# Upper weights of two matrix products placed 64 and 32 bytes beyond the common rest by 2048

## The chip, the cores and the metric

The kernel runs on one core of a Trainium2 chip. The metric is device time in microseconds, the median of several runs. A core has a matrix engine (TensorE, PE in the profile; its loads of the stationary operand are listed as PEld), a vector engine (VectorE, DVE), a scalar engine (ScalarE, ACT), a general engine (GpSimd, POOL) and a queue engine that starts DMAs (SyncE, SP). All read operands from the on-chip memory SBUF, which has 128 partitions; an address below is the byte within a partition, the same for all partitions.

## The reference

Attention in a sliding window of 64 positions, then a feed-forward layer with a normalized SoLU. Batch 8, 8 heads, 576 positions, head size 64; 4608 tokens, model width 512, hidden width 1024.

```python
def _attn_ref(q, k, v):
    scores = scale * np.matmul(q, k.transpose(0, 1, 3, 2))
    mask = (rel >= 0) & (rel < 64)
    scores = np.where(mask, scores, -1000000000.0)
    attn = softmax(scores)          # exp, sum, divide
    return np.matmul(attn, v)

def _moe_ref(x, w_in, w_out, g_ln):
    h = x @ w_in                    # 4608 x 512 @ 512 x 1024, the first product
    solu = h * softmax(h)
    ln = (solu - mean) / np.sqrt(var + 1e-06) * g_ln
    return ln @ w_out               # 4608 x 1024 @ 1024 x 512, the second product
```

## The kernel before

The tokens are cut into 36 tiles of 128. For each tile the kernel computes the scores (line 460), the softmax, the transposed probabilities, the attention's values (line 559), the first product (`moe_in`), the normalization (`moe_norm`), a transpose, and the second product (`moe_out`). All operations of all tiles go into a planner (`Plan`), which orders them by costs and due times that are written into the source; each engine's instructions are then emitted in that order. The planner knows no addresses.

The products run in three passes at a reduced 32-bit float form (`F32R`): an operand is split into an upper part, rounded to that form, and a lower part, the rest. The three passes are upper x upper, upper x lower and lower x upper. The first three tiles of the first product and the first two of the second run in plain fp32 instead (lines 590 and 724), while the split weights are still being made.

- Upper weights: `w_inH` ([128, 4, 1024], first product) and `w_outH` ([128, 8, 512], second product), 16384 bytes in each partition, both in the pool `const`. ACT writes them once (lines 392 and 397).
- Lower weights: `WL(i)`, eight of the sixteen uses of the ring `w` (nine tiles of 4096 bytes each); its other eight uses hold the weights in plain fp32.
- Activations: `xH`, `xL` (2048 bytes a tile), `yH`, `yL` (4096 bytes a tile), upper and lower, in rings of two.

In a matmul the activations are the stationary operand: 128 columns, 512 bytes in each partition, loaded by an instruction of their own (PEld). The weights are the moving operand: 512 columns, 2048 bytes, streamed past. For each pair of output halves (first product) or input chunks (second product) the order of passes is a group of six:

```python
        passes = [(c, d, *kinds[k]) for c in range(NC) for d, k in ((0, 0), (0, 1), (1, 0), (1, 1), (0, 2), (1, 2))]
```

so the streamed weights go upper, lower, upper, lower, upper, upper. In the first product `xH[:, c]` is the stationary operand of the first four and `xL[:, c]` of the last two. There are four groups per tile, 24 matmuls, in each product. Line 603 issues those of the first product, line 737 those of the second; 33 tiles go through line 603 and 34 through line 737.

Tiles lie in SBUF in the order in which they are first asked for: first the pool `const`, then the rings of the pool `sb` (`qk`, `raw`, `v`, `sS`, `w`, `PT`, `xH`, `e`, `sq`, `yH`, `xL`, `ot`, `yL`, `y`), then small columns. Two tiles of `const` are never used, `shift` and `gap`; they only take room:

```python
    const.tile([P, 272], F32, name="shift")
    w_inH = const.tile([P, NC, DFF], F32R, name="w_inH")
    w_outH = const.tile([P, NF, DM], F32R, name="w_outH")
    g_sb = const.tile([P, NF], F32, name="g_sb")
    const.tile([P, 240], F32, name="gap")
    neghalf = const.tile([P, 1], F32, name="neghalf")
```

`g_sb` holds the layer's scale, read when the second product's weights are split; `neghalf` is a constant of 4 bytes.

Of the kernel before, what the change touches and what calls it, by code (L numbers as in the profile page):

```python
# [9 lines left out]
F32 = mybir.dt.float32  # L10
# [9 lines left out]
P = 128  # L20
# [206 lines left out]
def tile_window_attention_solu_moe(  # L227
# [31 lines left out]
    const = ctx.enter_context(tc.tile_pool(name="const", bufs=1))  # L259
# [24 lines left out]
        if first is not None:  # L284
            nc.gpsimd.memset(t[first * WIN:(first + 1) * WIN, :WIN], NEG)

    const.tile([P, 272], F32, name="shift")
    w_inH = const.tile([P, NC, DFF], F32R, name="w_inH")
    w_outH = const.tile([P, NF, DM], F32R, name="w_outH")
    g_sb = const.tile([P, NF], F32, name="g_sb")  # L290
    const.tile([P, 240], F32, name="gap")
    neghalf = const.tile([P, 1], F32, name="neghalf")
    nc.gpsimd.memset(neghalf, -0.5)

# [605 lines left out]
```

## Time and profile before

| | |
|---|---|
| Median of three runs | 512.38 us (511.92 to 512.64) |
| Profiled execution, its own time | 513.01 us |
| Its span, first to last instruction | 510.9 us |
| PE busy | 492.1 us (96%), 4064 matmuls |
| PEld busy | 392.4 us (77%) |
| DVE busy | 409.8 us (80%) |
| ACT busy | 355.6 us (70%) |
| POOL busy | 314.5 us (62%) |
| DMA | 94.09 MB, 184 GB/s on average |
| Granted PE clock | 1.00 |

Busy times of different engines overlap, so they do not add up to the span. Matmuls overlap one another as well: the time that a matmul adds is the distance from its start to the next one's start (its pitch), not its listed duration. A group in the profile is named by source line, engine, operation, and output<-inputs.

### The profile page before, as it was taken

How to read it: one execution, taken by the hardware profiler on the slowest of the kernel's cores; microseconds unless marked ns; L12 is line 12 of the kernel's file. 1: busy time of each engine (PE TensorE's matmuls, PEld its weight loads, DVE VectorE, ACT ScalarE, POOL GpSimd, SP SyncE). 2: the span in 40 equal slices, each digit the busy share in tenths (PEclk: the TensorE clock that was granted, in tenths of full speed). 3: DMA queues.
4: the chain of work that ended last, by engine and by line, in shares of the span. 5: the costliest groups of instructions: out<-in, count | busy, mean ns of one | idle time of the engine just before them, and what ended most of it. 6: DMA issues, size and time to landing. Idle time of an engine off the chain costs nothing.

```text
span 510.9 us, 11601 instructions
## 1 busy us (share of the span) xinstructions
PE 492.1 (96%) x4064; PEld 392.4 (77%) x4064; DVE 409.8 (80%) x1176; ACT 355.6 (70%) x960; POOL 314.5 (62%) x566
## 2 busy tenths in 40 slices
PE   2889999999999999999999999999999999999996
PEld 1445577888788888888888888888888888888885
DVE  5998997888796989787978898887878878977531
ACT  4589795868686777777776868686859586865331
POOL 4388467664757475758574858584848485936430
PEclk9999999999999999999999999999999999999999
DMA  8994446966889989898889797879897969764301
GB/s 321 412 410 177 116 120 119 234 156 147 173 219 148 234 164 229 171 223 163 229 151 243 143 250 145 250 141 247 132 244 144 267 117 222 124 131 103 83 21 43
DMA packets 150762, 94.09 MB, mean 184 GB/s; under 512 B 135088, under 2 KB 135344, under 8 KB 150320
## 3 DMA queue, kind: packets, MB, share of 16 engines
q1 hardware_dynamic: 150704, 93.35, 76.7%
q8 instruction: 32, 0.52, 0.5%
q14 instruction: 26, 0.21, 0.1%
HBM read 50.86 MB, written 9.44 MB: 118 GB/s over the span
## 4 chain that ended last, share of the span: by engine, by line
PE 85%; DVE 4%; ACT 2%; POOL 2%; DMA 2%; issue 0%; SPq 0%; ACTq 0%; DVEq 0%; POOLq 0%
PE pH L603 34%; PE pO L737 34%; PE pO L559 6%; PE pS L460 6%; PE pO L724 3%; PE pH L590 1%; DMA raw<-raw 1%; ACT sS L480 1%; POOL sS L498 1%; PE pS L700 1%; DVE e L623 1%; DVE mst L618 1%; DMA y<-ot 1%; ACT e L620 0%; DVE w L368 0%
## 5 line engine op out<-in xcount | busy, mean ns | idle before, releaser
L498 POOL TENSOR_SCALAR sS<-sS,rec 128x128 f32<-128x128 f32 x280 | 149.2, 554 | 10.8 <-PE pS L460 7.4
L480 ACT ACTIVATE sS<-sS,nmx 128x128 f32<-128x128 f32 x288 | 111.5, 389 | 1.5 <-DVE nmx L475 1.4
L737 PE MATMUL pO<-w_outH,yH 128*128 128x512 f32 x272 | 108.2, 398 | 0.0
L737 PE MATMUL pO<-w,yH 128*128 128x512 f32 x272 | 106.1, 390 | 0.0
L603 PE MATMUL pH<-w_inH,xH 128*128 128x512 f32 x264 | 103.7, 393 | 0.8 <-DVE mst L623 0.8
L603 PE MATMUL pH<-w,xH 128*128 128x512 f32 x264 | 101.8, 389 | 0.0
L737 PE MATMUL pO<-w_outH,yL 128*128 128x512 f32 x272 | 83.9, 389 | 0.0
L512 ACT COPY raw<-sS 128x1024 uint16<-128x1024 uint16 x64 | 66.6, 1046 | 22.9 <-POOL sS L498 22.7
L603 PE MATMUL pH<-w_inH,xL 128*128 128x512 f32 x264 | 81.9, 389 | 0.0
L640 POOL TENSOR_SCALAR e<-e,mst 128x512 f32<-128x512 f32 x72 | 66.8, 936 | 3.9
L632 POOL TENSOR_SCALAR mst<-mst 128x1 f32<-128x1 f32 x36 | 19.9, 553 | 79.8 <-ACT sq L629 42.9
L522 DVE COPY PT<-raw 128x1024 uint16<-128x1024 uint16 x64 | 50.0, 789 | 19.9 <-DMA raw<-raw 19.7
L573 ACT CAST xH<-pO 128x512 fp32r<-128x512 f32 x33 | 19.3, 586 | 63.5 <-PE pO L559 63.4
L737 PEld LDWEIGHTS pO<-w_outH,yH 128*128 128x128 f32 x272 | 51.0, 188 | 12.7 <-issue 2.6
L618 DVE TENSOR_REDUCE mst<-pH 128x1 f32<-128x1024 f32 x36 | 44.0, 1221 | 20.1 <-PE pH L603 20.0
L737 PEld LDWEIGHTS pO<-w_outH,yL 128*128 128x128 f32 x272 | 51.1, 188 | 10.9
L603 PEld LDWEIGHTS pH<-w_inH,xH 128*128 128x128 f32 x264 | 49.6, 188 | 12.2 <-PE pO L737 1.2
L737 PEld LDWEIGHTS pO<-w,yH 128*128 128x128 f32 x272 | 51.1, 188 | 10.0
L603 PEld LDWEIGHTS pH<-w_inH,xL 128*128 128x128 f32 x264 | 49.6, 188 | 10.6 <-issue 0.2
L603 PEld LDWEIGHTS pH<-w,xH 128*128 128x128 f32 x264 | 49.6, 188 | 10.4 <-issue 0.2
L626 POOL TENSOR_SCALAR mst<-mst 128x1 f32<-128x1 f32 x36 | 18.9, 524 | 62.3 <-DVE mst L623 56.5
L629 ACT ACTIVATE sq<-e,mst 128x1024 bf16<-128x1024 f32 x36 | 41.4, 1150 | 21.6 <-POOL mst L626 21.6
(71 smaller groups left out, 852.3 us busy)
## 6 DMA issues: line engine op xcount, KB each, us to landing
qk<-qk SPq DMA_DIRECT2D x36, 640.0 KB, 5.9
v<-vS SPq DMA_DIRECT2D x36, 512.0 KB, 4.7
y<-ot SPq DMA_DIRECT2D x35, 256.0 KB, 2.7
raw<-w_out SPq DMA_DIRECT2D x4, 1024.0 KB, 12.0
raw<-w_in SPq DMA_DIRECT2D x3, 1024.0 KB, 11.5
raw<-raw SPq DMA_TRANSPOSE x126, 3.2
raw<-w_in SPq DMA_DIRECT2D x2, 512.0 KB, 6.2
y<-ot SPq DMA_DIRECT2D x2, 128.0 KB, 1.7
```

The costliest lines, as they stand in the source:

```text
L460: nc.tensor.matmul(PS(t, p // 2)[half * WIN:(half + 1) * WIN, r, p], q[rs, p, half * WIN:(half + 1) * WIN], keys, start=True, stop=True)
L480: plan.op("ACT", 390, lambda h=h: nc.scalar.activation(SS(t)[:, h], SS(t)[:, h], AF.Exp, bias=cols("nmx", h), scale=-1.0, accum_out=cols(" ...
L498: plan.op(engine, cost, lambda h=h: v.tensor_scalar(SS(t)[:, h], SS(t)[:, h], rec()[:, h:h + 1], 0.0, ALU.mult, ALU.add), [R], [("sS", t, ...
L512: plan.op("ACT", 1050, lambda x=x: nc.scalar.copy(XP(t)[:, x], SS(t)[:, 4 * x:4 * x + 4].bitcast(U16).rearrange("p h (n w) -> p w (h n)", ...
L522: plan.op("DVE", 740, lambda x=x: nc.vector.tensor_copy(PT(t)[:, 4 * x:4 * x + 4].bitcast(U16).rearrange("p h (n w) -> p h w n", w=2), XP( ...
L559: nc.tensor.matmul(PX(t, p)[r * D:(r + 1) * D, p, ks], V(t, half)[:, h * D:(h + 1) * D], PT(t)[:, h, ks], start=True, stop=True)
L603: plan.op("PE", 235, lambda n=n, c=c, d=d, x=x, w=w: nc.tensor.matmul(PH(t)[:, d * 512:(d + 1) * 512], x(t)[:, c], WH(c, d) if w is WH els ...
L618: plan.op("DVE", 1225, lambda: nc.vector.tensor_reduce(nmax(), PH(t), axis=AX.X, op=ALU.max, negate=True), [("pH", t)], [key(0)])
L629: plan.op("ACT", 1150, lambda: nc.scalar.activation(T("sq", t, [P, DFF], BF16), E(t), AF.Square, bias=nmean(), scale=1.0, accum_out=ss()), ...
L632: plan.op("POOL", 240, lambda: nc.gpsimd.tensor_scalar(kk(), ss(), se(), se(), ALU.mult, ALU.mult), [key(1), key(3)], [key(5)])
L640: plan.op("POOL", 770, lambda h=h, hs=hs: nc.gpsimd.tensor_scalar(E(t)[:, hs], E(t)[:, hs], nmean(), kk(), ALU.add, ALU.mult), [key(4), ke ...
L737: plan.op("PE", 235, lambda n=n, f=f, i=i, x=x, y=y, w=w: nc.tensor.matmul(PO(), y(t)[:, f], w(i, x), start=(n == 0), stop=(n == len(passe ...
```

## The change

Two of the unused tiles change their size, and a third is put between the two upper weights. `w_inH` then begins 64 bytes later than before, `w_outH` 2080 bytes later (32 beyond a multiple of 2048), and all that lies behind `gap` 2048 bytes later. Nothing else is edited; the instructions and their order stay as they are.

```diff
-    const.tile([P, 272], F32, name="shift")
+    const.tile([P, 288], F32, name="shift")
     w_inH = const.tile([P, NC, DFF], F32R, name="w_inH")
+    const.tile([P, 504], F32, name="between")
     w_outH = const.tile([P, NF, DM], F32R, name="w_outH")
     g_sb = const.tile([P, NF], F32, name="g_sb")
-    const.tile([P, 240], F32, name="gap")
+    const.tile([P, 232], F32, name="gap")
     neghalf = const.tile([P, 1], F32, name="neghalf")
```

## The prediction

> **What bounds the kernel now.** I read the page from the top: busy time by engine, granted clock, chain that ended last, groups of instructions.
>
> ```profile
> span 510.9 us, 11601 instructions
> PE 492.1 (96%) x4064; PEld 392.4 (77%) x4064; DVE 409.8 (80%) x1176; ACT 355.6 (70%) x960; POOL 314.5 (62%) x566
> PEclk9999999999999999999999999999999999999999
> PE 85%; DVE 4%; ACT 2%; POOL 2%; DMA 2%; issue 0%; SPq 0%; ACTq 0%; DVEq 0%; POOLq 0%
> ```
>
> TensorE (PE) is busy 96% of the span and is 85% of the chain that ended last, at full granted clock from the first slice to the last. In the middle of the run it never rests:
>
> ```profile
> core 0: us, PE busy (x) PEld busy (x) DVE busy (x) ACT busy (x) POOL busy (x), PEclk, DMA share, GB/s
> 210.00:310.00 100.00, 100.00 (x881) 83.50 (x880) 84.67 (x253) 73.03 (x207) 64.13 (x115) 1.00 0.88 193
> 310.00:410.00 100.00, 100.00 (x881) 83.49 (x880) 83.40 (x252) 72.62 (x197) 64.67 (x116) 1.00 0.89 198
> ```
>
> So a nanosecond more on a matmul in these stages is a nanosecond more on the whole, and one less is one less until another engine is the bound; VectorE (DVE), the next, has 15 us in 100 to spare. What fills PE is the two products with 512 columns, six groups (line, engine, operation, operands, form, count, then busy us and mean ns of one):
>
> ```profile
> L737 PE MATMUL pO<-w_outH,yH 128*128 128x512 f32 x272 | 108.2, 398 | 0.0
> L737 PE MATMUL pO<-w,yH 128*128 128x512 f32 x272 | 106.1, 390 | 0.0
> L603 PE MATMUL pH<-w_inH,xH 128*128 128x512 f32 x264 | 103.7, 393 | 0.8 <-DVE mst L623 0.8
> L603 PE MATMUL pH<-w,xH 128*128 128x512 f32 x264 | 101.8, 389 | 0.0
> L737 PE MATMUL pO<-w_outH,yL 128*128 128x512 f32 x272 | 83.9, 389 | 0.0
> L603 PE MATMUL pH<-w_inH,xL 128*128 128x512 f32 x264 | 81.9, 389 | 0.0
> ```
>
> These are 1608 matmuls. The mean of 389 ns is not what one costs, since they overlap; the cost is the distance from start to start, which the timeline shows (start us, duration us). One tile's whole first product, and the start of the next second product:
>
> ```profile
> 305.03 0.39 PE L603 MATMUL pH<-w_inH,xH 128*128 128x512 f32 x1
> 305.25 0.39 PE L603 MATMUL pH<-w,xH 128*128 128x512 f32 x1
> 305.48 0.39 PE L603 MATMUL pH<-w_inH,xH 128*128 128x512 f32 x1
> 305.71 0.39 PE L603 MATMUL pH<-w,xH 128*128 128x512 f32 x1
> 305.94 0.62 PE L603 MATMUL pH<-w_inH,xL 128*128 128x512 f32 x2
> 306.39 0.39 PE L603 MATMUL pH<-w_inH,xH 128*128 128x512 f32 x1
> ...
> 307.75 0.39 PE L603 MATMUL pH<-w_inH,xH 128*128 128x512 f32 x1
> ...
> 309.11 0.39 PE L603 MATMUL pH<-w_inH,xH 128*128 128x512 f32 x1
> ...
> 310.47 0.39 PE L737 MATMUL pO<-w_outH,yH 128*128 128x512 f32 x1
> ```
>
> From 305.03 to 310.47 there are 24 matmuls: 5.44 us / 24 = 226.7 ns each, and each group of six takes the same 1.36 us. 1608 x 226.7 ns = 364.5 us, 71% of the span. This pitch is the quantity that decides.
>
> **The change part by part.** It adds, removes and moves no instruction, wait, DMA or queue entry: the order is planned from costs that know no address. What changes is where three tiles lie. Adding up sizes: before, from the start of `w_inH` to the ring `w` there are 2 x 16384 bytes of upper weights, 32 of `g_sb`, 960 of `gap`, 32 for `neghalf` (4 bytes, taken as 32), 3 x 5120 of `qk`, 4 x 8192 of `raw`, 3 x 4096 each of `v` and `sS`: 106,496 bytes, 52 x 2048. So both upper weights, `w`, and behind it `xH`, `yH`, `xL`, `yL` all begin at one rest by 2048. Afterwards `w_inH` begins 64 bytes later, `w_outH` 64 + 2016 = 2080, that is 32 beyond the rest, `g_sb` 2080 later, and all behind `gap` 64 + 2016 - 32 = 2048 later, at the old rest. The new places stay multiples of 32.
>
> *Setting up the upper weights.* They are written by ScalarE (ACT) and read back by DVE once, early on:
>
> ```profile
> L392 ACT CAST w_inH<-w x8: 602/612/617, 41.5 to 54.1; 128x512 fp32r<-128x512 f32 x8
> L397 ACT ACTIVATE w_outH<-w,g_sb x8: 710/716/726, 56.5 to 70.1; 128x512 fp32r<-128x512 f32 x8
> ```
>
> 16 instructions, 8 x 0.612 + 8 x 0.716 = 10.6 us on ACT, which is 70% busy. Even 1% on them would be 0.1 us, under other work. I take zero.
>
> *Streaming the upper weights.* 264 + 264 + 272 + 272 = 1072 of the 1608 matmuls stream a shifted operand; the other 536 stream `w`. No row of before shows an upper weight at another rest, so this must be bounded.
>
> From below, the same 512 columns in plain fp32, while the kernel starts up, each with a weight load of its own:
>
> ```profile
> 35.54 7.03 PE L590 MATMUL pH<-w,xH 128*128 128x512 f32 x16
> L590 PE MATMUL pH<-w,xH x48: 592/592/1223, 16.1 to 53.4; 128*128 128x512 f32 x48
> L603 PEld LDWEIGHTS pH<-w_inH,xH x264: 186/188/190, 63.5 to 487.0; 128*128 128x128 f32 x132
> ```
>
> (7.03 - 0.59) / 15 = 429 ns a record, half of it 214.6. If the newer form is worth exactly twice as much a column, its pitch of 226.7 holds 12.1 ns beyond streaming. A cause at hand is the load of the next weights, 188 ns long, which runs beside the stream and reads the same memory. Were it wholly due to the common rest, 1072 x 12.1 ns = 13.0 us would go.
>
> From above, the slowest pitch of such a stream in this trace, behind a burst of small matmuls:
>
> ```profile
> 299.79 0.39 PE L737 MATMUL pO<-w,yH 128*128 128x512 f32 x1
> 300.02 0.39 PE L737 MATMUL pO<-w_outH,yH 128*128 128x512 f32 x1
> ...
> 300.94 0.39 PE L737 MATMUL pO<-w_outH,yH 128*128 128x512 f32 x1
> 301.18 0.39 PE L737 MATMUL pO<-w,yH 128*128 128x512 f32 x1
> 301.40 0.39 PE L737 MATMUL pO<-w_outH,yH 128*128 128x512 f32 x1
> ```
>
> From 299.79 to 301.18 there are six: 231.7 ns, 5.0 more than in the rows above with the same operands. 1072 x 5.0 ns = 5.4 us would come on top.
>
> Which end is nearer? Two readings say neither. First, the stationary operand moves while the moving one always starts at the same rest: `xH[:, c]` begins 512 bytes further for each c, so the four groups at 305.03, 306.39, 307.75 and 309.11 put the two reads 0, 512, 1024 and 1536 bytes apart, and all take 1.36 us. A conflict that hung on the rest by 2048 or 1024 would show as a difference between them. One with a shorter period is met by the weight load several times on its 512 bytes, at whatever place it starts, so a shift by 32 or 64 moves the meetings and hardly changes their number. Second, what else uses the memory does not matter:
>
> ```profile
> 305.03:306.39 1.36, 1.36 (x8) 1.13 (x6) 1.33 (x5) 1.36 (x8) 1.36 (x3) 1.00 0.31 65
> 309.11:310.47 1.36, 1.36 (x8) 1.13 (x6) 0.86 (x2) 1.14 (x2) 1.36 (x4) 1.00 1.01 189
> ```
>
> DVE is busy 1.33 us in one group and 0.86 in another, DMA moves 65 and 189 GB/s, and both take 1.36. The pitch looks like something PE does by itself. So I take 0 ns, with +5.0 and -12.1 as ends.
>
> The Trainium skill, "SBUF — State Buffer", section "Who interferes with whom", gives PE two independent read ports, one for the moving operand and one for weight loads, and says that PE never waits on anyone. By it the sum is zero too; the trace agrees as far as the two rows just shown go, and the rule leaves the 12.1 ns unexplained. Against it stands "TensorE: Matmul & The Clock Gate", section "Back-to-back issue gap", of the Trainium skill: 512 / 2.4 + 2.5 ns, about 216, for 512 columns. As an estimate from that page, 1072 x (226.7 - 216) ns = 11.5 us would be the most that the shift frees.
>
> Sum: 0 + 0, against the profiled execution's own 513.01 us (span 510.9 and 2.1 around it). That execution is 0.63 us above the median of the runs shown, 512.38, so I forecast 512.4.
>
> **The rivals.** *The common rest costs something and the shift takes part of it away.* Place: each of the 1072 records. For it: 12.1 ns a record are unaccounted for, and two pitches with the same operands (226.7, 231.7) show that the pitch is not fixed by the columns alone. Against it: the four equal groups. With half of the excess gone, 1072 x 6.05 ns = 6.5 us, it gives 505.9; whole, 499.4. It counts from 1 ns a record on (1.07 us). Nothing would take it back before DVE's 15% is used up.
>
> *The common rest is what keeps the stream smooth, and the shift breaks it: slower.* With one rest, the last byte of one stream is followed, by 2048, by the first of the next: the addresses run on in a ring across all matmuls. Afterwards four of the six transitions in a group (upper to lower weights and back) jump by 64 or 32 bytes. For it: before has every stream at one rest and shows the same pitch for all six kinds. Against it: the weights' own start jumps by 512 at every step without a trace of it. Price: up to the 231.7 of the interrupted stream, 5.0 ns on 1072 records, 5.4 us: 517.8. It decides from 1 ns a record on.
>
> *The change doesn't do what it says*, if a size were rounded otherwise than I added it: then all relations shift by the same unknown amount, and the time is again that of one of the cases above. It has no chance of its own.
>
> **How the numbers follow.** From no change a measurement of this kernel can tell about 0.2%, 1.0 us: the three runs span 511.92 to 512.64. No change: 0.40, time 512.4, its own range 511.4 to 513.4. Faster: 0.36; smaller shares of the excess are likelier than half, so about 0.26 of it lies above 505.9. Slower: 0.24, with about 0.14 below 516.0. From 505.5 to 516.0 the range holds 0.40 + 0.26 + 0.14 = 0.80. The likeliest case sets the time, though it holds less than half.
>
> **What would show it.** Right: in the changed kernel the 24 matmuls of a first product and of a second product again take 5.44 us from start to start, and the three kinds in a group have one pitch. Faster rival: a group of six under 1.36 us, with the shortened steps where `w_inH` or `w_outH` streams, or where the load beside them runs. Slower rival: steps over 227 ns where upper and lower weights follow each other, while the step between the last two of a group, both upper, stays. If only one product changes, the offset (64 or 32) is what matters, not the common rest. The prediction is wrong if the pitch moves by 1 ns or more, in either direction; the setting up (16 ACT instructions at 0.61 and 0.72 us) should be as before in any case.

## The result, and the profile after

| | before | changed |
|---|---|---|
| Median | 512.51 us (511.92 to 512.88, 4 runs) | 519.81 us (519.64 to 520.08, 4 runs) |
| Profiled execution, its own time | 513.01 us | 520.08 us |
| Its span | 510.9 us | 517.9 us |

The changed kernel is slower: ratio 1.0138, 95% interval 1.0125 to 1.0151, 7.3 us more. The forecast was 512.4, the range 505.5 to 516.0.

One line was added to the source, so line 603 of before is 604 here and 737 is 738. The page's busy time by engine, and the six groups of the products:

```profile
PE 497.9 (96%) x4064; PEld 391.8 (76%) x4064; DVE 407.1 (79%) x1176; ACT 355.5 (69%) x960; POOL 313.9 (61%) x566
L738 PE MATMUL pO<-w_outH,yH 128*128 128x512 f32 x272 | 109.3, 402 | 0.0
L738 PE MATMUL pO<-w,yH 128*128 128x512 f32 x272 | 107.4, 395 | 0.0
L604 PE MATMUL pH<-w_inH,xH 128*128 128x512 f32 x264 | 104.6, 396 | 0.0
L604 PE MATMUL pH<-w,xH 128*128 128x512 f32 x264 | 103.0, 394 | 0.0
L738 PE MATMUL pO<-w_outH,yL 128*128 128x512 f32 x272 | 85.3, 395 | 0.0
L604 PE MATMUL pH<-w_inH,xL 128*128 128x512 f32 x264 | 83.4, 394 | 0.0
```

Counts are the same, the other engines are as busy as before or a little less, and PE has 5.8 us more. The mean listed duration of all six kinds is 3 to 6 ns longer, of those that stream the unmoved `w` too. The timeline of one first product and one second product (start us, duration us) shows where:

```profile
308.17 0.39 PE L604 MATMUL pH<-w_inH,xH 128*128 128x512 f32 x1
...
313.74 0.39 PE L738 MATMUL pO<-w_outH,yH 128*128 128x512 f32 x1
...
316.52 0.40 PE L738 MATMUL pO<-w_outH,yH 128*128 128x512 f32 x1
316.76 0.40 PE L738 MATMUL pO<-w,yH 128*128 128x512 f32 x1
317.00 0.39 PE L738 MATMUL pO<-w_outH,yH 128*128 128x512 f32 x1
317.23 0.39 PE L738 MATMUL pO<-w,yH 128*128 128x512 f32 x1
317.46 0.63 PE L738 MATMUL pO<-w_outH,yL 128*128 128x512 f32 x2
...
319.32 0.39 PE L604 MATMUL pH<-w_inH,xH 128*128 128x512 f32 x1
```

24 matmuls of the first product take 313.74 - 308.17 = 5.57 us (232.1 ns each) in place of 5.44; of the second 319.32 - 313.74 = 5.58 us (232.5). The steps, all 226 or 227 ns before, now differ: from 316.52 on they are 0.24, 0.24, 0.23 and 0.23 us.

The chain that ended last has most products in one piece each (start us, us). A second product behind small matmuls, a first product, and a second product behind it:

```profile
144.12 5.77 PE pO L738 x24
149.89 5.57 PE pH L604 x24
155.46 5.58 PE pO L738 x24
```

In the kernel before, the same chain had for the two second products:

```profile
143.77 5.67 PE pO L737 x24
154.88 5.44 PE pO L737 x24
```

So 33 x 0.13 us in the first product, and 14 x 0.14 (behind a first product) and 17 x 0.10 (behind small matmuls) in the second, make 4.3 + 2.0 + 1.7 = 8.0 us; the other three second products stand in the chain in other pieces. The groups of before had one wait of 0.8 us (for DVE's `mst`) that is now 0.0: 7.2 us, against 7.0 in the spans.

### The profile page after: what moved, and what is told of

The parts are those of the page before. It is cut to its first block, busy times and chain, and to the rows that moved or that the text cites. A ratio compares the mean times of both kernels' runs of the same rounds, so it can differ in the third digit from the quotient of the medians.

```text
span 517.9 us, 11601 instructions
## 1 busy us (share of the span) xinstructions
PE 497.9 (96%) x4064; PEld 391.8 (76%) x4064; DVE 407.1 (79%) x1176; ACT 355.5 (69%) x960; POOL 313.9 (61%) x566
## 4 chain that ended last, share of the span: by engine, by line
PE 90%; POOL 2%; ACT 1%; DVE 1%; issue 0%; ACTq 0%
PE pO L738 37%; PE pH L604 35%; PE pO L560 6%; PE pS L461 6%; PE pO L725 3%; PE pH L591 1%; POOL sS L499 1%; PE pS L701 1%; ACT sS L481 1%; POOL mst L627 0%; DVE w L394 0%; DVE yL L712 0%; POOL raw L361 0%; ACT sq L630 0%; ACT yH L710 0%; DVE e L624 0%
## 5 line engine op out<-in xcount | busy, mean ns | idle before, releaser
L499 POOL TENSOR_SCALAR sS<-sS,rec 128x128 f32<-128x128 f32 x280 | 146.2, 541 | 11.2 <-PE pS L461 7.4
L738 PE MATMUL pO<-w_outH,yH 128*128 128x512 f32 x272 | 109.3, 402 | 0.0
L738 PE MATMUL pO<-w,yH 128*128 128x512 f32 x272 | 107.4, 395 | 0.0
L604 PE MATMUL pH<-w,xH 128*128 128x512 f32 x264 | 103.0, 394 | 0.0
L738 PE MATMUL pO<-w_outH,yL 128*128 128x512 f32 x272 | 85.3, 395 | 0.0
L604 PE MATMUL pH<-w_inH,xL 128*128 128x512 f32 x264 | 83.4, 394 | 0.0
L641 POOL TENSOR_SCALAR e<-e,mst 128x512 f32<-128x512 f32 x72 | 68.7, 963 | 3.9
L738 PEld LDWEIGHTS pO<-w,yH 128*128 128x128 f32 x272 | 51.1, 188 | 12.1
```

Source lines behind the costliest of these rows:

```text
L499: plan.op(engine, cost, lambda h=h: v.tensor_scalar(SS(t)[:, h], SS(t)[:, h], rec()[:, h:h + 1], 0.0, ALU.mult, ALU.add), [R], [("sS", t, ...
L604: plan.op("PE", 235, lambda n=n, c=c, d=d, x=x, w=w: nc.tensor.matmul(PH(t)[:, d * 512:(d + 1) * 512], x(t)[:, c], WH(c, d) if w is WH els ...
L641: plan.op("POOL", 770, lambda h=h, hs=hs: nc.gpsimd.tensor_scalar(E(t)[:, hs], E(t)[:, hs], nmean(), kk(), ALU.add, ALU.mult), [key(4), ke ...
L738: plan.op("PE", 235, lambda n=n, f=f, i=i, x=x, y=y, w=w: nc.tensor.matmul(PO(), y(t)[:, f], w(i, x), start=(n == 0), stop=(n == len(passe ...
```

## The experiments

Three theories on what an operand's place does. *Distance*: what counts is how far, by some period, the streamed address lies from that of the weight load beside it. *Jump*: what counts is how far one stream's address lies from the one before. *Place*: what counts is where an operand lies by itself.

**One product at a time.** First product only:

```diff
-    const.tile([P, 272], F32, name="shift")
+    const.tile([P, 288], F32, name="shift")
     ...
+    const.tile([P, 496], F32, name="between")
     ...
     const.tile([P, 240], F32, name="gap")
```

> Only the upper weights of the first product begin 64 bytes beyond the common rest; those of the second are back on it. Three theories: (pair) what counts is the distance between the address that is streamed and the address of the weight load running beside it; (jump) what counts is the step of the streamed address, by 2048, from one matmul to the next; (place) what counts is where an operand lies by itself, a multiple of 2048 being bad. All three expect the first product slow (24 matmuls in about 5.57 us from start to start, as in the changed kernel) and the second back at 5.44 us: 33 x 0.13 = 4.2 us of the 7 remain, about 516.5 us. If the two shifts only cost together, about 512.5.

Second product only:

```diff
     const.tile([P, 272], F32, name="shift")
     ...
+    const.tile([P, 8], F32, name="between")
     ...
-    const.tile([P, 240], F32, name="gap")
+    const.tile([P, 232], F32, name="gap")
```

> Only the upper weights of the second product begin 32 bytes beyond the common rest. Pair, jump and place alike: the second product's 24 matmuls take 5.58 us without an interruption and 5.68 behind small matmuls, the first product's 5.44; 14 x 0.14 + 17 x 0.095 = 3.6 us remain, about 516 us. Without an effect of the 32 bytes, 512.5.

Measured: 516.54 us (ratio 1.0067, 1.0037 to 1.0096) and 516.91 us (1.0080, 1.0043 to 1.0116). The chain of the first, then of the second:

```profile
123.40 5.58 PE pH L604 x24
128.99 5.44 PE pO L738 x24
```

```profile
128.63 5.58 PE pO L738 x24
149.37 5.46 PE pH L604 x24
```

Each shift slows its own product and leaves the other near 5.44. The kernel before took 512.7 us beside them: the two lose 3.8 and 4.2 us apart and 7.3 together, so the losses nearly add up. Neither 64 nor 32 is the harmless one.

**All operands later by 64.** `shift` has 288 columns, `gap` 240, `between` is left out, so the weights, and all tiles behind, lie 64 bytes later.

> All operands, stationary and streamed ones, lie 64 bytes later than in the kernel before, so the common rest by 2048 is kept and is now zero. Pair and jump: nothing changes between operands, the pitch is 226.7 ns again and the time 512.5 us. Place: the first product's upper weights lie at the same place as in the changed kernel, so at least its part stays, 516 us or more.

Measured: 512.20 us (ratio 0.9985, 0.9968 to 1.0002).

```profile
122.75 5.44 PE pH L603 x24
128.19 5.44 PE pO L737 x24
```

`w_inH` lies exactly where it lies in the changed kernel, and nothing is lost. So the theory of place fails: what counts is how the operands lie to one another.

**Streams by themselves.** The first probe runs 51 streams of 36 matmuls, each with its own offsets:

```python
off = d if m == "H" else 0               # m: "H" upper, "L" lower; order H L H L H H
last = d if n and steps[n - 1][2] == "H" or not n else 0
mo = off if what in ("upper", "jump") else 0             # shift of the stream
so = {"upper": 0, "load": d, "jump": last, "pair": -last}[what]   # of its own load
```

> Computes none of the reference: it is only streams of 36 matmuls in the kernel's order of upper and lower weights (upper, lower, upper, lower, upper, upper), back to back, on one core. Each stream has its own offsets: 'upper' shifts only the upper weights by d bytes, 'load' only the stationary operand, 'jump' shifts the upper weights and each load that runs beside them, so that the distance of the two stays and only the steps between streams remain, and 'pair' leaves all streams on one rest and shifts each load so that its distance to the stream beside it is that of 'upper'. At offset zero all theories expect 226.7 ns a matmul. Pair: 'pair' by 32, 64, 128 is as slow as 'upper' (230 to 234 ns), 'jump' is 227. Jump: 'jump' is as slow as 'upper', and 'pair' and 'load' are 227 throughout. Place: both 'upper' and 'jump' slow by where the address lies, 'load' too. If a constant distance is harmless at every offset, 'load' stays at 227 ns; if some distances are better than zero, it shows which.

In the timeline a stream is one row (start us, us); the distance to the next row, by 36, is its pitch. Some of them, in this order: `upper` 64, `load` 64, `jump` 64 and `pair` 64, each followed by the next stream's start:

```profile
67.79 8.53 PE L61 MATMUL pb<-big 128*128 128x512 f32 x36
76.17 8.48 PE L61 MATMUL pa<-big 128*128 128x512 f32 x36
...
233.68 8.55 PE L61 MATMUL pb<-big 128*128 128x512 f32 x36
242.08 8.50 PE L61 MATMUL pa<-big 128*128 128x512 f32 x36
...
374.58 8.50 PE L61 MATMUL pa<-big 128*128 128x512 f32 x36
382.92 8.45 PE L61 MATMUL pb<-big 128*128 128x512 f32 x36
391.21 8.45 PE L61 MATMUL pa<-big 128*128 128x512 f32 x36
```

(76.17 - 67.79) / 36 = 232.8 ns for `upper` 64; 233.3 for `load` 64; 231.7 for `jump` 64 and 230.3 for `pair` 64. The first step of a stream still belongs to the one before; the mean over the last three groups of each, in ns:

| offset, bytes | 0 | 16 | 32 | 64 | 96 | 128 | 192 | 256 | 384 | 512, 1024, 1536 |
|---|---|---|---|---|---|---|---|---|---|---|
| upper | 226.7 | 230.3 | 233.3 | 232.2 | 232.2 | 230.6 | 228.9 | 226.7 | 230.6 | 226.7 |
| load | 226.7 | 233.3 | 233.3 | 233.3 | 234.4 | 232.1 | 228.9 | 226.7 | 232.0 | 226.7 |

The offsets left out of the table took 230 to 235 ns, but for -64 (228.9 in both series) and `load` -16 (226.7). The period is 256 bytes as far as these offsets show: 256 is as good as 0, 384 much like 128, and 192 like -64. Distance by itself costs: `load` has no jump of the stream. The jump costs too: in `jump` the load keeps its distance from the stream beside it, and is still slow. Neither theory alone covers both series (a rival to this reading stands with the third probe). In the changed kernel both happen, and the streams of upper weights by 64 and 32 (232.2 and 233.3) match its 232.1 and 232.5 ns.

How much is each? `pair` has the change's distances with no stream moved, and by the same mean took 230.2 at 64 and 233.3 at 32; `jump` has the change's jumps with the distances kept, and took 231.8 and 232.2. Either by itself gives most of the loss, and the two don't add up.

**The period, in the kernel.** `shift` 336 columns and `gap` 176 put both upper weights 256 bytes beyond.

> Upper weights of both products begin 256 bytes beyond the rest of the others. In the streams measured by themselves an offset of 256, 512 or 1024 bytes ran at 226.7 ns, like zero. If the rest by 256 is what counts, this is as fast as the kernel before: 512.5 us. If it is the rest by 2048, as the source's sizes suggest, it is as slow as the changed kernel or slower: 1072 x 3 to 6 ns, 516 to 519 us.

Measured: 512.49 us (ratio 1.0008, 0.9994 to 1.0021). The chain shows 5.44 for both products:

```profile
122.65 5.44 PE pH L603 x24
128.09 5.44 PE pO L737 x24
```

The rest by 2048, on which the kernel's pads seem to be laid out, is stricter than needed.

**The loads alone, both ways.** A tile of 64 bytes (16 columns), or of 1984 (496 columns), ahead of `xH` in its pool, so that the stationary operands, and whatever else lies behind it there, lie 64 bytes after or before the weights' rest:

```diff
     def XH(t):
+        if ("pad", 0) not in plan.tiles:
+            plan.tiles["pad", 0] = sb.tile([P, 16], F32, tag="pad", name="pad", bufs=1)
```

> All weights, upper and lower, keep one rest, as in the kernel before; the stationary operands (xH, xL, yH, yL) begin 64 bytes later. No streamed address jumps. Jump alone: 512.5 us. Distance between stream and load: 'load' by 64 took 233.3 ns by itself, 1608 x 6.6 ns = 10.6 us more, 523 us.

> The same with the stationary operands 64 bytes before the common rest (1984 later). Jump alone: 512.5 us. Distance: 'load' by -64 took 228.9 ns by itself, 1608 x 2.2 ns = 3.6 us more, 516 us; if the sign of the distance did not matter, 523 as with +64.

Measured: 521.63 us (ratio 1.0178, 1.0145 to 1.0210) and 515.38 us (1.0055, 1.0034 to 1.0075). The chains, +64 and then -64:

```profile
129.24 5.60 PE pO L739 x24
```

```profile
129.66 5.49 PE pO L739 x24
```

5.60 / 24 = 233.3 and 5.49 / 24 = 228.8 ns, the probe's 233.3 and 228.9. No weight was moved: a distance of +64 alone makes the kernel slower than the change under study did, and the sign matters. (In the changed kernel the loads lie before the upper weights, so the distance there is -64 in the first product and -32 in the second.) Against the kernel before beside them (512.14 us) they lose 9.5 and 3.2 us, a little less than 1608 matmuls by the probe's loss (10.6 and 3.5): behind small matmuls the stream of before has not reached 226.7 yet, so there is less to lose (5.79 us a product with the loads at +64, against 5.67).

**Without the pads.** `shift` and `gap` deleted.

> The two unused tiles of the kernel before are left out. Its upper weights then begin 1088 bytes before the rest of the others, which is 192 beyond it by 256. If the rest by 256 decides and the streams measured by themselves carry over, the pitch is that of 'upper' by 192, 228.9 ns: 1608 x 2.2 ns = 3.6 us more, 516 us. If only offsets under some hundred bytes matter, 512.5 us.

Measured: 515.72 us (ratio 1.0066, 1.0041 to 1.0091), with 5.49 us a product, 228.8 ns:

```profile
133.88 5.49 PE pH L601 x24
```

So the pads of before gain about 3 us, by the alignment that the change gives up.

**Finer offsets, narrower loads, plain fp32.** The second probe:

```python
cols = {"half": 64, "quarter": 32}.get(what, P)          # columns of the stationary operand
kind = F32 if what[:5] == "plain" else F32R
```

> Computes none of the reference: streams as in the first probe. 'load': all streams on one rest, the stationary operand shifted by -64 to 64 bytes in steps of 4; a lower pitch than 226.7 ns would point to a faster kernel. 'half' and 'quarter': the stationary operand has 64 or 32 columns, so that the load beside the stream reads a half or a quarter. If the load's reads cost the 12 ns beyond 214.6, the pitch falls towards 220 and 217; if they are a fixed cost of a change of weights, it stays at 226.7. 'plain': fp32 in place of the rounded form; at 429 ns a record the stream reads half as fast. If the cost comes from two reads at full speed, an offset of 64 changes nothing there; if any shift costs, it is slower than 429.

Rows in order: `half` 0, `quarter` 0, and the start of the next; then `plain` 0, `plain upper` 0, `plain` 64, `plain upper` 64:

```profile
302.69 8.44 PE L58 MATMUL pb<-big 128*64 128x512 f32 x36
310.96 8.50 PE L58 MATMUL pa<-big 128*32 128x512 f32 x36
319.30 8.54 PE L58 MATMUL pb<-big 128*64 128x512 f32 x36
...
352.46 15.61 PE L58 MATMUL pb<-big 128*128 128x512 f32 x36
367.91 15.61 PE L58 MATMUL pa<-big 128*128 128x512 f32 x36
383.36 15.61 PE L58 MATMUL pb<-big 128*128 128x512 f32 x36
398.81 15.61 PE L58 MATMUL pa<-big 128*128 128x512 f32 x36
```

A load of half the columns gives 229.7 ns, of a quarter 231.7, and at the offsets 64 and 96 no stream with such a load fell under 226.6 either. So fewer bytes in the load do not shorten the pitch. Plain fp32 takes 15.45 / 36 = 429.2 ns at offset 0 and at 64 alike. Of the 33 constant distances from -64 to 64 bytes none is under 226.7 ns, and all but -64, -16, -4 and 0 are 230 to 237. Each ran behind the one 4 bytes below it, which matters (see the last section). So no offset tried points to a kernel faster than the one before.

**Other lengths, a steady walk, and what came before.** The third probe:

```python
cols = what if isinstance(what, int) else 512            # columns of the stream
if what == "walk":
    mo, so = n * d, (n - 1) * d
```

> Computes none of the reference: streams as in the first two probes. Numbers name the columns of a stream (480 to 256 in place of 512): if the 12 ns beyond streaming are a fixed cost of each matmul, the pitch at offset 0 is columns / 2.4 + 13.3 ns (213.3, 200, 173.3, 146.7, 120); if the streams lock to the memory's period of 256 bytes, the pitch does not fall in a straight line, and lengths that are no multiple of 64 columns behave like a jump. 'walk' moves each stream by d bytes against the one before and each load with the stream beside it: if the jump by itself costs, 16 to 128 are slow and 256 is 226.7; if the distance alone counts, all are 226.7. The series of 'load' repeats -16 and -4 behind different streams: in the first probe -16 ran at 226.7 and in the second at 228.2, so if the state that a stream begins in matters, its pitch depends on what came before.

Rows of 320 columns at 0 and 64, 256 at 0 and 64, and the next; then `walk` 128 and `walk` 256; then `load` -16, 64, -16, 0, -4, 64, -4, 0 (a `load` 0 stands before the first):

```profile
69.58 5.43 PE L60 MATMUL pa<-big 128*128 128x320 f32 x36
74.86 5.44 PE L60 MATMUL pb<-big 128*128 128x320 f32 x36
80.14 4.48 PE L60 MATMUL pa<-big 128*128 128x256 f32 x36
84.45 4.41 PE L60 MATMUL pb<-big 128*128 128x256 f32 x36
88.69 8.35 PE L60 MATMUL pa<-big 128*128 128x512 f32 x36
...
121.85 8.45 PE L60 MATMUL pa<-big 128*128 128x512 f32 x36
130.13 8.36 PE L60 MATMUL pb<-big 128*128 128x512 f32 x36
...
146.49 8.32 PE L60 MATMUL pb<-big 128*128 128x512 f32 x36
154.65 8.56 PE L60 MATMUL pa<-big 128*128 128x512 f32 x36
163.05 8.38 PE L60 MATMUL pb<-big 128*128 128x512 f32 x36
171.28 8.33 PE L60 MATMUL pa<-big 128*128 128x512 f32 x36
179.44 8.32 PE L60 MATMUL pb<-big 128*128 128x512 f32 x36
187.60 8.56 PE L60 MATMUL pa<-big 128*128 128x512 f32 x36
196.00 8.56 PE L60 MATMUL pb<-big 128*128 128x512 f32 x36
204.40 8.33 PE L60 MATMUL pa<-big 128*128 128x512 f32 x36
```

`walk` 128 is (130.13 - 121.85) / 36 = 230.0, with the distance of each load to the stream beside it kept, and `walk` 256 settles at 226.7: the jump costs at a constant distance too, and at 256 it doesn't. One rival is left. In `walk` and `jump` a load keeps its distance to the stream that runs beside it, but not to the stream of its own matmul, which comes next; a rule that a load must agree with both would make these series slow without a jump, and no run here separates the two.

At offset 0 a stream of 320 columns takes (74.86 - 69.58) / 36 = 146.7 ns and one of 256 columns 119.7. From 320 to 512 columns the pitch grows by (226.7 - 146.7) / 192 = 0.417 ns a column; at that rate 512 columns take 213.3 and 320 take 133.3, so 13.4 ns a matmul come on top. The last three groups of 384 columns have 173.3 (13.3 on top), but 448 and 480 have 202.7 and 216.7 with uneven steps, 16.0 and 16.7 on top: a length, too, can break the short pitch, and not only one that is no multiple of 64.

## Why the prediction was wrong

*What bounds the kernel, what the change moves, which quantity decides*: right. PE's pitch went from 226.7 to 232 ns, and it came out as span almost one to one.

*The step that failed* is the choice of 0 ns between the two ends, by its first reading. The four equal groups at 0, 512, 1024 and 1536 bytes were read as a sign that the relation of addresses doesn't matter. All four are multiples of 256, the distances at which nothing changed in any run. The reading was true and said nothing on 32 and 64. The second half of it, that a shorter period would be met equally often from any start, is refuted: a constant distance of +64 costs 6.6 ns a matmul. In place of 0 ns, products that nothing interrupts took 5.4 ns a matmul more in the first product and 5.8 more in the second. The Trainium skill's rule beside it ("SBUF — State Buffer", "Who interferes with whom": PE's two read ports are independent and PE waits on no one) agrees with this trace as to DMA and the other engines (a group of six took 1.36 us at 65 and at 189 GB/s). It does not hold between PE's own two streams (226.7 ns, and 233.3 with the loads 64 bytes further), and there the measurement decides.

*The rival that came true* is the slower one: 517.8 forecast, 519.81 measured. Its mechanism is part of it. It named the jump between streams, and `jump` 64 and 32 take 231.8 and 232.2 ns. The argument against it, a start that jumps by 512 without a trace, falls like the four groups: 512 is a multiple of 256. It had no term for the distance of the loads, which by itself gives 230.2 and 233.3 (`pair`). In the first product the loads lie on the cheap side: 64 bytes before every stream cost 2.1 ns a matmul (228.8), so most of the 5.4 ns there would come of the alternation from matmul to matmul. The term of its sum that was off is the count. It charged 1072 matmuls, and predicted that the step between two upper streams stays. In the products that nothing interrupts, the mean step became longer at all six places of a group, and between the two upper streams it rose from 226.8 to 233.5 ns in the first product and to 230.0 in the second. Single steps go from 225 to 241 ns. At the forecast 5.0 ns, 1608 matmuls would have been 8.0 us, against 7.3 measured.

*The upper bound of 231.7 ns* was taken from the stream behind small matmuls, as the slowest pitch at hand. Nothing tied it to offsets, and that it lies so near to the measured 232.1 and 232.5 is luck as far as the runs show. The first probe's first stream, at offset 0, passes through similar steps (231, 236, 228, 232, 231 ns, after a start at 427) before it falls to 226.7. Whether shifted streams are held in that state is not shown.

*The faster rival* had the 12.1 ns from a load that reads beside the stream. Narrower loads do not shorten the pitch of 512 columns, and no offset tried does: none fell under 226.6, so the 216 of the estimate beside it was not reached either. What this part of the pitch is stays open.

## What to carry to other kernels

Where matmuls of the reduced 32-bit form with 512 columns follow each other, with a load of 128 columns each, put every streamed tile and every stationary tile at one rest by 256 bytes. The pads cost room and, here, no time (512.20 and 512.49 us with moved operands at one rest), and an offset of 64 bytes on one kind of operand cost 0.6 to 1.8%. When a trace shows no dependence on some offset, ask which offsets it holds: steps of 512 bytes say nothing about 64. A short program of streams with chosen offsets gave the kernel's pitch within 1 ns.

## What the runs showed of the hardware

The pitch depends on what came before, not only on the addresses. In the third probe `load` -16 takes (154.65 - 146.49) / 36 = 226.7 ns behind `load` 0, and 228.6 behind `load` 64; `load` -4 takes 226.7 behind 0, and 233.3 behind 64; `load` 16 had 233.3 in the first probe and 226.7 here. So a small offset kept the short pitch behind a stream at the common rest, and mostly not behind a shifted one (`load` -4 behind -8 did, in the second probe). `half` at offset 96 ran at 226.7 too, while `half` at 0 did not.

Plain fp32, at about half the speed, took 429.2 ns at offset 0 and at 64, the only one tried. And 256 columns at offset 64, (88.69 - 84.45) / 36 = 117.8 ns, were faster than at 0 (119.7), so the rule of one rest is shown for 512 columns only. What has a period of 256 bytes, and why a distance and a jump break the short pitch, no run here shows.
